# Issuing every second transfer of a layer border from ScalarE, with the Relu on VectorE

## The chip, the cores and the metric

The kernel runs on one core of one Trainium2 chip. A core has TensorE (matrix products, whose results go to the accumulator banks called PSUM), VectorE, ScalarE and GpSimd for elementwise work, SyncE for issuing transfers, and 16 DMA engines that bring data from the chip's memory (HBM) to the on-chip memory (SBUF, 128 partitions). Each engine works through its own list of instructions in order; they meet through semaphores. SyncE and ScalarE can both issue transfers; the profile calls their queues q1 and q10.

The metric is the time of one execution in device microseconds, the median of several runs. The changed kernel is compared with this one.

## What is computed

Two layers over a batch of two single tokens (decoding), each an attention block over a long cache and a gated feed-forward block. The second layer uses the same weights and the same cache as the first.

```python
def _A_ref(x, k_cache, v_cache, wq, wo):          # x: 2 x 1 x 512
    q = (x @ wq) -> 32 heads of 128
    k, v = each of 8 cached heads serves 4 query heads   # cache: 2 x 8 x 32768 x 128, each
    p = softmax(q k^T * 128 ** -0.5)
    return (p v) @ wo
def _B_ref(x, W_gate, W_up, W_down):              # 512 -> 1792 -> 512
    gate = x @ W_gate; gate = gate * (gate > 0)
    return (gate * (x @ W_up)) @ W_down

x = x + _A_ref(_layernorm(x), ...); x = x + _B_ref(_layernorm(x), ...)   # twice
```

All data are fp32. Each layer reads the whole cache of keys and values, 16 groups (8 heads by 2 tokens) of 16 MB of keys and 16 MB of values, except for the part that the second layer finds still on the chip.

## The kernel before

**Places on the chip.** One large SBUF tile, `arena`, holds nearly everything. Its first three parts, X, Z and Y, are slots of 16384 columns (8 MB) for one half of a group's keys or values each. Behind them, partly over the end of Y, lies a **ring** (`RING`) of 6752 columns, 3.46 MB, through which the small weight transfers of the border pass. `ring(width)` gives the next place and begins again at the start when the end is reached.

**The laps.** In a layer, 16 laps each take one group: keys in two halves, a softmax (`soft_max`, whose Exp is ScalarE's work), values in two halves. The second layer takes the groups in the opposite order, so that the key half that the first layer had last can be used again.

**The border.** Between the last lap of the first layer and the first of the second lies a chain that needs little data but in strict order: the last values, the output projection, the feed-forward block, and the queries of the next layer. `feed_forward` reads the weights `wgu` (gate and up) in 32 units of 448 columns, the first 16 for the gate and the others for up, cut into pieces by `UNITS[0]` = 4, 3, 3, 3, 1, 3, 3, 2, 1, 3, 1, 2, 3 units; then `wd` (down) in pieces by `DOWN[0]` = 4, 3, 3, 3, 1 blocks of 512 columns. `queries` then reads `wq` in 17 pieces by `QUERY`, 3, 2, 2, 2, 2, 1 and so on, 32 blocks of 512 columns. Each piece goes to the ring, so its transfer waits until TensorE has used what lay there. After the queries the rest of the kept key half is completed by the four `AGAIN` transfers (line 661).

**Who issues.** `fetch` (line 353) records one transfer. A caller may name the semaphore (`lane`); if not, the next of 16 lanes is taken and the counter `turn[2]` goes up by one. All transfers are SyncE's (line 358), but for the two loads of x at the start, which are ScalarE's (line 372). `turn` (line 339) is the list of counters: place in `stat`, place in the ring, lanes, start of the ring.

**The order around the change.** Every instruction is recorded on a `Tape`, which works out for each one which semaphores it has to wait for: what wrote its inputs, and what still reads the place it writes. What an engine has waited for already is not waited for again. Each engine then runs its own list in the recorded order. Line 214 is where every recorded instruction is given out, so nearly all rows of the profile bear that line, and tiles tell the work apart.

**The Relu.** In `feed_forward`, after the 16 gate units (`e == 15`, line 582), the gate's sums in the bank `acc` are scaled by the layer norm's factor `rs` and cut at zero by one ScalarE instruction (line 583) into `gh`. The up sums, in the bank `op`, are multiplied on by VectorE after all 32 units (line 586). Between, TensorE runs a few matmuls of constants into idle banks (`warm`).

Of the kernel before, what the change touches and what calls it, by code (L numbers as in the profile page):

```python
# [6 lines left out]
AF = mybir.ActivationFunctionType  # L7
ALU = mybir.AluOpType
# [11 lines left out]
FS = F // 4  # L20
# [13 lines left out]
X, Z, Y, FLOW = 0, ROW, 2 * ROW, 3 * ROW  # L34
# [3 lines left out]
RING = Y + ROW - STASH, FLOW + 3840  # L38
# [18 lines left out]
UNITS = (4, 3, 3, 3, 1, 3, 3, 2, 1, 3, 1, 2, 3), (16, 8, 8)  # L57
# [251 lines left out]
def attention_reglu_decode(nc, hold, x, k, v, wq, wo, wgu, wd, out):  # L309
    tape = Tape(nc)  # L310
    pe, dve, act, pool, sp = map(tape.engine, ("tensor", "vector", "scalar", "gpsimd", "sync"))
# [17 lines left out]
    def tile(at, width):  # L329
        return arena[:, at : at + width]  # L330
# [5 lines left out]
    mhalf, mean_cols = cst[:, C_HALF : C_HALF + NB], cst[:, C_MEAN : C_MEAN + 1]  # L336


    turn = [0, FLOW, 0, RING[0]]

    def one():
        turn[0] = (turn[0] + NB) % 32
# [5 lines left out]
    def ring(width):  # L348
        at = turn[1] if turn[1] + width <= RING[1] else turn[3]
        turn[1] = at + width  # L350
        return at

    def fetch(at, src, lane=None, also=()):
        t = arena[:, at : at + src.shape[-1]]
        if lane is None:
            lane = f"lane{turn[2] % LANES}"
            turn[2] += 1
        sp.dma_start(t, src, lane=lane, also=also)
        return t

    def half(src, n, h, at, also=()):
# [28 lines left out]
    def warm(width, bank=acc):  # L390

        pe.matmul(bank[:32, :width], pair, mean_cols.to_broadcast([P, width]), start=True, stop=True)
# [31 lines left out]
    def spread(tot, rows, w, start, stop):  # L424
        for c in range(4):
            pe.matmul(tot[32 * c : 32 * c + rows.shape[-1], :P], rows, w[:, c * P : (c + 1) * P], start=start, stop=stop)
# [137 lines left out]
    def feed_forward(last, total):  # L564
        xT, ss = centred(total, not last)
        gh, hT = tile(WIDE_AT, FS), tile(XT_AT, FS)
        up = acc, op
        begins = {sum(UNITS[last][:e]): n for e, n in enumerate(UNITS[last])}
        for e in range(8 * KT):
            if e in begins:  # L570
                n = begins[e]
                t, at = fetch(X + e * FS if last else ring(n * FS), wgu[:, e * FS : (e + n) * FS]), e
            s, kt, j = e // 16, e // 4 % 4, e % 4
            pe.matmul(up[s][32 * j : 32 * j + 32, :FS], xT[:, kt, :], t[:, (e - at) * FS : (e - at + 1) * FS],
                      start=kt == 0, stop=kt == KT - 1)
            if e == 3:
                rs = factor(ss, True)
            if last and e in (15, 23):
                warm(448, scores[:, 0, :])
            elif not last and e in (23, 27):  # L580
                warm(224)
            if e == 15:
                act.activation(gh, up[0][:, :FS], AF.Relu, scale=rs[:, 0:1])
        warm(448)
        for a, e in ((0, 256), (256, FS)):
            dve.scalar_tensor_tensor(gh[:, a:e], up[1][:, a:e], rs[:, 0:1], gh[:, a:e], ALU.mult, ALU.mult)
            dve.transpose(hT[:, a:e], gh[:, a:e])
        rows = hT.rearrange("p (a b) -> p a b", b=32)
        tot = small[1]
        c = 0  # L590
        for n in DOWN[last]:
            t = fetch(Z + c * D if last else ring(n * D), wd[:, c * D : (c + n) * D])
            for e in range(c, c + n):
                spread(tot, rows[:, e, :], t[:, (e - c) * D : (e - c + 1) * D], e == 0, e == NC - 1)
            c += n
            if c in ((4, 8) if last else (4, 7, 10)):
                warm(448)
            elif last and c in (10, 12):
                warm(224)
        return add(tot, last)  # L600
# [3 lines left out]
    for L in range(NLAYER):  # L604
        last = L == NLAYER - 1
        step = -1 if last else 1
        seq = list(range(NG))[::step]


        a, c, b = (X, Z, Y) if not last else (Z, X, Y)  # L610

        weights, other = [tile(WO_AT + at * WO, WO) for at in ((1, 0) if last else (0, 1))]

        def keys(h, t, first=0, scores=scores):
            for e in range(0, t.shape[-1] // D, 8):
                k_blocks(h + e, t[:, e * D : min(t.shape[-1], (e + 8) * D)], first, scores)
                yield e

        def values(lo, t, first=False, final=False):
            n = t.shape[-1] // D  # L620
            for e in range(0, n, 8):
                v_blocks(lo + e, lo + min(e + 8, n), t[:, e * D : min(e + 8, n) * D], first and e == 0, final and e + 8 >= n)

        def lap(i, second, k_first):

            values(HALF, second or half(v, seq[i - 1], 1, b), False, True)
            evacuate(False)
            for e in keys(0, k_first or half(k, seq[i], 0, a, (weights,) if i > L else ())):
                if e == 8:
                    head_out(1, tile(ACS_AT, D), weights)  # L630
            if not last and i == NG - 1:
                pool.tensor_copy(tile(RING[1], KEPT), tile(a, KEPT))
            for _ in keys(HALF, half(k, seq[i], 1, c)):
                pass
            soft_max()
            soft_tail()
            values(0, half(v, seq[i], 0, a), True)
            place_queries(seq[L] + step, step)
            if i % 2 == 1 and i > 1 and (last or i + 1 < NG):
                h = seq[i] // NB  # L640
                if h == 0:
                    fetch_out(h, 1, weights)
                elif i % 4 == 3:
                    fetch_out(h - last, 2, tile(WO_AT, 2 * WO))
                else:
                    pool.tensor_copy(weights, other)

        kept = keys(HALF, tile(a, ROW), NT // 2, gu) if last else iter(())
        queries(L, total, seq[0], kept)
        dve.memset(oT, 0.0)  # L650
        for _ in kept:
            pass
        nothing(op, True)
        ready = {}
        if last:
            n, e = divmod(KEPT, D)

            def again(col):
                return a + col - KEPT if col < REST * D else RING[0] + LENT + col - REST * D

            for lo, hi in AGAIN:
                fetch(again(lo), k[seq[0], 0, :, lo:hi])
            k_blocks(0, tile(RING[1], n * D), NT // 2, gu)
            k_blocks(n, tile(RING[1] + n * D, e), NT // 2, gu, (0, e))
            k_blocks(n, tile(again(KEPT), D - e), NT // 2, gu, (e, D))
            for lo in range(n + 1, HALF):
                for _ in range({12: 3, REST: 2, 26: 2}.get(lo, 0)):
                    warm(448)
                if lo == REST + 4:
                    put_back(LENT, STASH)  # L670
                k_blocks(lo, tile(again(lo * D), D), NT // 2, gu)
            ready = {1: (tile(b, ROW), half(k, seq[1], 0, a))}
            fetch_out(seq[0] // NB, 1, weights)
            warm(448)
            warm(448)
            soft_max(gu)
            soft_tail()
            values(0, tile(c, ROW), True)
            place_queries(seq[1])
        else:  # L680
            ready = {0: (tile(b, ROW), None)}
            fetch_out(0, 1, weights)
            dve.memset(tile(PT_AT, 2 * D), 0.0)
            nothing(acc, True)
        for i in tape.laps(range(L, NG), 1):
            lap(i, *ready.pop(i, (None, None)))
        nothing(op, False)
        combine()
        n = seq[NG - 1]
        for lo, hi in ENDING if last else FLOWN:  # L690
            t = fetch(b + lo * D, v[n, 1, :, lo * D : hi * D])
            if not last and hi == TAIL:
                v_halves(HALF + lo, t)
            else:
                values(HALF + lo, t, False, last and lo >= 28)
            if not last and lo == TAIL:
                for at, bank in stash():
                    dve.tensor_copy(bank, tile(RING[0] + at, bank.shape[-1]))
        if not last:
            warm(SPARE[1], small[1])  # L700
            warm(SPARE[1], small[1])
        head_out(n % NB, evacuate())
        if not last:
            warm(SPARE[1], small[1])
        project(weights if last else fetch_out(n // NB, 1, tile(ring(WO), WO), None), True)
        total = feed_forward(last, add(op))
    sp.dma_start(out, xq, lane="out")
    tape.write()
# [30 lines left out]
```

## Time and profile before

| | |
|---|---|
| median of three runs | 2558.35 us (2557.49 to 2558.69) |
| the profiled execution: own time, span in the trace | 2558.98 us, 2557.7 us |
| granted TensorE clock over the span | 0.751 |
| busy: TensorE, VectorE, ScalarE, GpSimd | 52%, 6%, 2%, 1% |
| bytes read | 1102.76 MB |
| chain that ended last: waiting for keys, for values | 37%, 34% |
| the border: the first `wgu` piece issued, last `wq` piece issued | 1272.23 us, 1325.20 us |
| ScalarE: last Exp before the border, Relu, next Exp | 1252.27, 1292.47, 1352.95 us |

A row of the groups and of the timeline names a line, an engine, an operation, and its result and inputs by tile (`acc<-arena` is a product of data in `arena` into the bank `acc`); `x64` is the count. SPq and ACTq are instructions of SyncE and ScalarE that issue transfers; their time is that of the issue, not of the transfer. A time in square brackets is how long the engine had stood idle before that row, and for whom. In a list of waits the three numbers are the total in us, how many times, and the longest. In the rows of issues stand the count, the size of each, and the median time from issue to the last byte's landing. "DMA share" is the mean busy share of the 16 DMA engines; a packet is counted where it starts, so in a short window the share can be a little over 1.

### The profile page before, as it was taken

How to read it: one execution, taken by the hardware profiler on the slowest of the kernel's cores; microseconds unless marked ns; L12 is line 12 of the kernel's file. 1: busy time of each engine (PE TensorE's matmuls, PEld its weight loads, DVE VectorE, ACT ScalarE, POOL GpSimd, SP SyncE). 2: the span in 40 equal slices, each digit the busy share in tenths (PEclk: the TensorE clock that was granted, in tenths of full speed). 3: DMA queues.
4: the chain of work that ended last, by engine and by line, in shares of the span. 5: the costliest groups of instructions: out<-in, count | busy, mean ns of one | idle time of the engine just before them, and what ended most of it. 6: DMA issues, size and time to landing. Idle time of an engine off the chain costs nothing.

```text
span 2557.7 us, 20577 instructions
## 1 busy us (share of the span) xinstructions
PE 1337.5 (52%) x9546; PEld 366.1 (14%) x9546; DVE 156.3 (6%) x405; ACT 60.3 (2%) x82; POOL 18.5 (1%) x25
## 2 busy tenths in 40 slices
PE   4554545455444554455586554455545554455456
PEld 1111111111111111111121111111111111111112
DVE  1000000000000000000111000000000000000001
ACT  0000000000000000000000000000000000000000
POOL 0000000000000000000000000000000000000000
PEclk9677777777776777777798777777777777777778
DMA  9999999999999999999999999999999999999999
GB/s 425 429 440 428 437 430 436 434 429 440 429 440 427 438 430 430 439 429 440 420 403 440 432 436 431 433 436 431 437 430 437 430 434 435 433 436 431 437 430 390
DMA packets 27391, 1103.06 MB, mean 431 GB/s; under 512 B 3048, under 2 KB 3568, under 8 KB 8304
## 3 DMA queue, kind: packets, MB, share of 16 engines
q1 hardware_dynamic: 27360, 1102.84, 99.9%
q8 instruction: 12, 0.20, 0.0%
q14 instruction: 3, 0.02, 0.0%
q10 hardware_dynamic: 16, 0.00, 0.0%
HBM read 1102.76 MB, written 0.07 MB: 431 GB/s over the span
## 4 chain that ended last, share of the span: by engine, by line
DMA 73%; PE 25%; issue 0%; SPq 0%; DVE 0%; ACT 0%; ACTq 0%
DMA arena<-k 37%; DMA arena<-v 34%; PE acc L214 12%; PE pair L214 11%; DMA arena<-wd 1%; PE op L214 1%; PE small L214 1%; DMA arena<-wq 1%; DMA arena<-wgu 0%; SPq L214 0%; DVE arena L214 0%; DVE stat L214 0%; DVE xq L214 0%; ACT arena L214 0%; ACTq L295 0%
## 5 line engine op out<-in xcount | busy, mean ns | idle before, releaser
L214 PE MATMUL acc<-arena 128*16 128x512 f32 (+2 forms) x4292 | 612.7, 726 | 530.7 <-DMA arena<-v 519.9
L214 PE MATMUL pair<-arena,qz 128*32 128x512 f32 x4098 | 593.8, 732 | 557.9 <-DMA arena<-k 557.9
L214 PEld LDWEIGHTS pair<-arena,qz 128*32 128x32 f32 x4098 | 151.8, 131 | 989.0 <-issue 702.1
L214 PEld LDWEIGHTS acc<-arena 128*16 128x16 f32 (+1 forms) x4292 | 136.9, 112 | 970.2 <-issue 594.9
L214 ACT ACTIVATE arena<-pair,stat 128x1024 f32<-128x1024 f32 x32 | 35.6, 1113 | 2390.2 <-DVE stat L214 2390.2
L214 DVE TENSOR_SCALAR arena<-acc,stat 128x512 f32<-128x512 f32 (+2 forms) x35 | 25.0, 719 | 1049.0 <-PE acc L214 1049.0
L214 DVE TENSOR_REDUCE stat<-pair 128x1 f32<-128x1024 f32 x32 | 39.2, 1224 | 635.9 <-PE pair L214 635.9
L214 DVE STREAM_TRANSPOSE arena<-arena 128x512 f32<-128x512 f32 (+1 forms) x68 | 43.4, 674 | 40.8 <-ACT arena L214 40.7
L214 PE MATMUL small<-stat,cst 128*128 128x1 f32 (+1 forms) x72 | 17.0, 305 | 48.6 <-ACT arena L214 48.6
L214 PE MATMUL small<-arena,cst 128*128 128x32 f32 x64 | 13.1, 287 | 51.6 <-DVE arena L214 51.6
L214 PEld LDWEIGHTS small<-cst,arena 128*128 128x128 f32 x264 | 31.9, 191 | 29.5 <-issue 27.3
L214 PE MATMUL small<-cst,arena 128*128 128x4 f32 x264 | 34.8, 255 | 1.1 <-DVE arena L214 1.1
L214 PE MATMUL op<-arena,oT 128*2 128x512 f32 (+1 forms) x312 | 34.4, 526 | 0.4 <-DVE oT L214 0.3
L214 DVE MEMSET oT<- 128x8 f32 x33 | 2.1, 65 | 513.0 <-PE op L214 513.0
L214 POOL COPY arena<-arena 128x2048 f32<-128x2048 f32 (+1 forms) x7 | 13.8, 1972 | 2191.8 <-PE op L214 2046.8
L214 PE MATMUL op<-arena 128*32 128x448 f32 (+1 forms) x128 | 22.9, 573 | 4.2 <-DMA arena<-wgu 2.0
L214 PEld LDWEIGHTS small<-stat,cst 128*128 128x128 f32 x72 | 13.9, 242 | 56.9 <-ACT arena L214 52.2
L214 PEld LDWEIGHTS small<-arena,cst 128*128 128x128 f32 x64 | 9.5, 188 | 80.5 <-DVE arena L214 80.5
L214 ACT ACT_TABLE_LOAD x16 | 20.5, 1283 | 11.2 <-DMA xq<-x 10.9
L214 PE MATMUL acc<-cst 128*32 128x448 f32 (+1 forms) x48 | 18.3, 480 | 0.0
L214 PE MATMUL small<-cst,stat 128*128 128x2 f32 x8 | 1.7, 287 | 18.4 <-DVE stat L214 17.8
L214 PE MATMUL small<-arena 128*32 128x128 f32 x224 | 8.7, 277 | 2.8 <-DMA arena<-wd 2.2
(63 smaller groups left out, 98.9 us busy)
## 6 DMA issues: line engine op xcount, KB each, us to landing
arena<-wo SPq DMA_DIRECT2D x6, 2048.0 KB, 31.9
arena<-v SPq DMA_DIRECT2D x2, 4096.0 KB, 37.8
arena<-wq SPq DMA_DIRECT2D x13, 512.0 KB, 6.2
arena<-wgu SPq DMA_DIRECT2D x7, 672.0 KB, 6.3
arena<-wo SPq DMA_DIRECT2D x4, 1024.0 KB, 25.7
arena<-wgu SPq DMA_DIRECT2D x1, 3584.0 KB, 44.7
arena<-wgu SPq DMA_DIRECT2D x2, 1792.0 KB, 49.0
arena<-v SPq DMA_DIRECT2D x2, 1536.0 KB, 41.9
```

Source lines behind the costliest of these rows:

```text
L214: ins = getattr(engine, op.call)(*args, **op.kw)
```

## The change

Three things are changed. `turn` gets a fifth entry, a switch, which `feed_forward` puts on in the first layer when it reaches the fifth piece of `wgu` (`sum(UNITS[0][:4])` is unit 13), and which is put off just ahead of the `AGAIN` transfers. While it is on, `fetch` gives a transfer without a lane of its own to ScalarE when the lane counter is odd, else to SyncE as before. And the Relu, in both layers, is a VectorE instruction: times `rs`, then the larger of that and zero.

```diff
-    turn = [0, FLOW, 0, RING[0]]
+    turn = [0, FLOW, 0, RING[0], False]
...
     def fetch(at, src, lane=None, also=()):
         t = arena[:, at : at + src.shape[-1]]
+        by = sp
         if lane is None:
             lane = f"lane{turn[2] % LANES}"
             turn[2] += 1
-        sp.dma_start(t, src, lane=lane, also=also)
+            if turn[4] and turn[2] % 2:
+                by = act
+        by.dma_start(t, src, lane=lane, also=also)
         return t
...
         for e in range(8 * KT):
+            if e == sum(UNITS[0][:4]):
+                turn[4] = not last
             if e in begins:
                 n = begins[e]
                 t, at = fetch(X + e * FS if last else ring(n * FS), wgu[:, e * FS : (e + n) * FS]), e
...
             if e == 15:
-                act.activation(gh, up[0][:, :FS], AF.Relu, scale=rs[:, 0:1])
+                dve.tensor_scalar(gh, up[0][:, :FS], rs[:, 0:1], 0.0, ALU.mult, ALU.max)
...
+            turn[4] = False
             for lo, hi in AGAIN:
                 fetch(again(lo), k[seq[0], 0, :, lo:hi])
```

## The prediction

> **What bounds the kernel now.** I read the page first: where the bytes go, and the chain that ended last.
>
> ```profile
> q1 hardware_dynamic: 27360, 1102.84, 99.9%
> ...
> q10 hardware_dynamic: 16, 0.00, 0.0%
> HBM read 1102.76 MB, written 0.07 MB: 431 GB/s over the span
> ...
> DMA 73%; PE 25%; issue 0%; SPq 0%; DVE 0%; ACT 0%; ACTq 0%
> ```
>
> One queue, SyncE's (q1), keeps the 16 DMA engines busy for 99.9% of the span; q10, which carried only the two loads of x, is ScalarE's. The kernel is a stream of bytes, so an edit counts only if the DMA engines stand idle, or take longer over the same bytes, for more or less time than now.
>
> Next I cut the trace into windows: a stretch of the steady laps, then the border between the layers. The last two columns are the busy share of the DMA engines and their GB/s.
>
> ```profile
> core 0: us, PE busy (x) PEld busy (x) DVE busy (x) ACT busy (x) POOL busy (x), PEclk, DMA share, GB/s
> 1100.00:1178.00 78.00, 38.82 (x276) 10.38 (x276) 4.76 (x13) 3.04 (x4) 0.00 (x0) 0.76 1.00 432
> 1288.00:1296.00 8.00, 5.48 (x32) 0.87 (x26) 0.00 (x0) 0.63 (x1) 0.00 (x0) 1.00 1.00 382
> 1316.00:1320.00 4.00, 3.42 (x16) 0.57 (x14) 0.38 (x1) 0.00 (x0) 0.00 (x0) 1.00 0.96 326
> 1330.00:1344.00 14.00, 13.42 (x92) 4.45 (x88) 1.20 (x4) 0.00 (x0) 0.00 (x0) 1.00 1.00 415
> 1283.00:1330.00 47.00, 37.74 (x330) 11.93 (x321) 7.01 (x27) 0.63 (x1) 1.26 (x2) 1.00 1.01 399
> ```
>
> The changed issues lie between 1283 and 1330. There the engines are busy as everywhere (1.01), yet move 399 GB/s against 432. Only 1316 to 1320 shows a share under 1 (0.96) and 326 GB/s: the one place where the queue looks almost empty. This gives the **most the change can bring**. The 47 us moved 47 x 399 = 18.75 MB, which at 432 GB/s take 43.4 us, 3.6 less; the 14 us at 415 would take 13.45, 0.55 less. Together 4.15 us, 0.16% of the time. The first bound lies inside what a measurement of this kernel can tell from no change, about 0.2% or 5.1 us.
>
> What holds the border's transfers back is in the waits of SyncE between 1283 and 1330: for whom, us in total, times, longest.
>
> ```profile
> SPq L214 <- PE op L214: 22.3, 13, 5.9
> SPq L214 <- PE acc L214: 7.9, 8, 1.4
> SPq L214 <- PE small L214: 7.6, 6, 1.9
> SPq L214 <- PE pair L214: 2.3, 1, 2.3
> ```
> SyncE waits 22.3 + 7.9 + 7.6 + 2.3 = 40.1 of the 47 us for TensorE to free a place of the ring; TensorE, busy 37.74, is idle 9.3 of them, as it uses each piece once it lands. It is a circle: land, use, free, issue, land. Only when its round is too long for the bytes in flight do the DMA engines run dry.
>
> **The change, part by part.** The moved part is 9 gates' pieces (19 units of 224 KB), 5 of `wd` (14 of 256 KB) and 17 of `wq` (32 of 256 KB): 31 transfers, 16,032 KB. The lane counter stands at 11 on the first, so the odd ones go to ScalarE: 16 transfers. SyncE keeps 15.
>
> First, the time of an issue. Where one release of TensorE frees two places, SyncE now issues them one behind the other.
>
> ```profile
> 1283.41 0.80 SPq L214 DMA_DIRECT2D arena<-wgu  x2
> ```
> ```profile
> 1315.01 0.80 SPq L214 DMA_DIRECT2D arena<-wq  x2
> ```
> ```profile
> 1283.41 0.33 SPq L214 DMA_DIRECT2D arena<-wgu  x1
> ```
>
> There are seven such couples between 1283 and 1325, the first and the last shown, each about 0.8 us long. One issue that waited takes 0.33 us, so the second stands some 0.4 us behind the first, and with two issuers it need not. It gains only where the DMA engines are waiting for it, which the windows show at 1316 to 1320 alone, right behind the couple of 1315.01. Value: **-0.4 us**; ends: 0 and 7 x 0.4 = -2.8.
>
> Second, the order in which data land. Now a piece lands whole before the next one begins. With two queues on the same engines the pieces may come by turns. The only traffic on q10 in this trace shows it.
>
> ```profile
> 1.08 9.67 ACTq L214 DMA_DIRECT2D xq<-x  x2
> ```
> ```profile
> q10 hardware_dynamic: 4, 0.00, 0.7%
> ```
> ```profile
> q10 hardware_dynamic: 4, 0.00, 0.5%
> ```
>
> The second row is of the window 7 to 8 us (the four data rows of 512 B), the third of 9.5 to 10 (the four small completion writes); from 8 to 9.5 nothing of q10 started. So 1 KB issued at 1.08 is done only near 10, and a big row of SyncE's queue came in between its data and its completion write. This is taking turns row by row. Two equal pieces that start together then land together, at the end of both: the earlier is late by up to its own length, and in a steady alternation by half of it. A 512 KB piece takes 1.31 us at 399 GB/s and one of 672 KB 1.72, so half is **0.66 to 0.86 us**.
>
> Is that covered? From issue to landing, median, and the shortest of the border (issued into the empty moment at 1315.01):
>
> ```profile
> arena<-wq SPq DMA_DIRECT2D x13, 512.0 KB, 6.2
> arena<-wgu SPq DMA_DIRECT2D x7, 672.0 KB, 6.3
> ```
> ```profile
> arena<-wq SPq DMA_DIRECT2D x1, 512.0 KB, 4.4
> ```
>
> A usual piece spends 6.2 - 4.4 = 1.8 us standing in the queue. A landing that is 0.66 to 0.86 later eats under half of this, so the engines still find work; it is hidden, except at the dry moment, where one half piece, **+0.7 us**, is paid. An issue by ScalarE may also be longer than SyncE's: the one row of it is of small transfers.
>
> ```profile
> L214 ACTq DMA_DIRECT2D xq<-x x2: 514/802/1090, 1.1 to 10.2; - x2
> ```
>
> That is 0.18 to 0.76 us over 0.33. With 0.86 it comes to 1.62, still under 1.8: nothing where there is a queue.
>
> [...]
>
> Third, the border's end. The first transfer of the kept-over key half (1712 KB) now stands on SyncE behind the last `wq` piece.
>
> ```profile
> 1325.20 0.33 SPq L214 DMA_DIRECT2D arena<-wq  x1
> ```
> ```profile
> 1325.57 0.43 SPq L214 DMA_DIRECT2D arena<-k  x1
> ```
> ```profile
> arena<-k SPq DMA_DIRECT2D x1, 1712.0 KB, 9.2
> ...
> arena<-k SPq DMA_DIRECT2D x1, 1536.0 KB, 16.4
> ```
> ```profile
> 1340.57 2.76 PE L214 MATMUL pair<-arena,qz 128*32 128x512 f32 x18 [0.58 <-DMA arena<-k]
> ...
> 1348.77 1.48 PE L214 MATMUL pair<-arena,qz 128*32 128x512 f32 x10 [1.56 <-DMA arena<-k]
> ```
>
> With that piece on ScalarE, the key transfer no longer waits behind it. It has eight rows per engine of 13,696 B against eight of 4,096, so by turns the piece could land behind all of it: 1712 KB / 399 GB/s = 4.4 us late at worst. TensorE has 0.58 + 1.56 = 2.1 us of waiting in store behind it. The rest delays only the softmax; the DMA engines hold keys by then (the 1536 KB take 3.9 us by rate and land after 16.4, so 12 us of queue), and nothing is paid in bytes: 0, at worst +2.3.
>
> Fourth, the Relu, once in each layer.
>
> ```profile
> 1292.47 0.63 ACT L214 ACTIVATE arena<-acc,stat 128x448 f32<-128x448 f32 x1 [38.99 <-PE op L214]
> ```
> ```profile
> L214 DVE TENSOR_SCALAR arena<-acc,stat 128x512 f32<-128x512 f32 x31 | 23.3, 750 | 1033.1 <-PE acc L214 1033.1
> L214 DVE TENSOR_SCALAR arena<-acc,stat 128x384 f32<-128x384 f32 x2 | 1.2, 617 | 15.8 <-PE acc L214 15.8
> ```
> ```profile
> DVE arena L214 <- PE op L214: 14.4, 1, 14.4
> ```
> ```profile
> DVE arena L214 <- PE op L214: 7.8, 1, 7.8
> ```
>
> Halfway between the VectorE rows, 128x448 takes about 0.68 us against 0.63. VectorE then waits 14.4 us (first layer) and 7.8 us (second) for the up half, so it is hidden: 0. Without that cover it would be 0.05. It also clears ScalarE: left there, it would stand between the transfers, as ScalarE takes its instructions in order. Nothing else of ScalarE's lies among them: it had idled 38.99 us before that Relu, and its next Exp needs the keys behind the border.
>
> **Sum**: -0.4 + 0.7 + 0 + 0 = +0.3 us on the profiled execution, 2558.98 to 2559.3. That execution lies 0.63 above the median of the three runs (2558.35), so the forecast is 2558.35 + 0.3, about **2558.6**.
>
> **The rivals.** (a) *The second queue fills the slow moments*: with two queues an engine has another row at hand whenever one arrives late. For it: a share of 1.00 at 382 GB/s, so the rows themselves are slow. Against it: half the pieces still come only when TensorE frees a place. It can win back at most the 4.15; half, -2.1, gives 2556.3.
>
> (b) *The round becomes too long* (the slower side): pieces by turns land half a piece later, and if the 1.8 us of standing are not there every round pays. Bytes in flight are 399 GB/s x 6.2 us = 2.47 MB, so 18.75 MB are 7.6 rounds; times 0.66 to 0.86 that is 5.0 to 6.5, mean 5.8: 2564.1. It decides from the point at which the time from issue to landing falls to 4.4 us plus the delay. For it: only 382 GB/s at 1288 to 1296. Against it: a share of 1.00 there. [...]
>
> (c) *The change does not do what it says*: each transfer waits for TensorE anyway, so two issuers are no faster than one and turns cost nothing: 2558.35.
>
> **How the numbers follow.** The forecast (from -1 to +1.5 around now) 0.50, (c) 0.14, (a) 0.19, (b) 0.17. Faster by over 0.2% would need more than the 4.15 us: 0.03. Of (b) about half lies beyond +5.1: slower 0.08. Within 0.2%: 0.89. The range takes in most of (a) and the milder part of (b): -2.9 to +4.2 around the median, 2555.5 to 2562.5.
>
> **What would show each step.** The queue rows: q10 with some 8.4 MB (8,160 KB). The windows: 1316 to 1320 over 326 GB/s if the couple counted, 1288 to 1296 near 382 if turns are hidden; both above 400 proves (a), and a share under 0.95 in several windows proves (b). The landing times: by turns, `wq` and `wgu` pieces go from 6.2 to about 7, the last `wq` piece far more, and the first key transfer is issued before 1325. The VectorE Relu should take 0.68 us with no one waiting. It would all be wrong if the end moved by over 5 us: then some lap outside the border has changed, which no row here foresees.

## The result, and the profile after

The changed kernel takes **2569.04 us** (median of 5 runs, 2568.13 to 2571.89) against 2558.35 (median of 5, 2557.49 to 2562.27) for the kernel before on the same chip: 10.7 us or 0.42% slower, ratio 1.0042 with a 95% interval of 1.0028 to 1.0057. The forecast was 2558.6, in a range of 2555.5 to 2562.5, with 0.08 on slower by over 0.2%.

The page of the changed kernel shows the transfers on the two queues as intended: 8.36 MB on ScalarE's q10.

```profile
q1 hardware_dynamic: 25056, 1094.48, 98.8%
q10 hardware_dynamic: 2320, 8.36, 0.9%
```

Where the time went is read from two windows, first of the kernel before, then of the changed one (columns as above; the last two are the DMA share and GB/s).

```profile
1288.00:1344.00 56.00, 46.88 (x368) 14.63 (x366) 6.78 (x22) 0.63 (x1) 0.70 (x1) 1.00 1.01 401
1344.00:1360.00 16.00, 11.78 (x73) 3.49 (x69) 5.39 (x11) 1.21 (x2) 0.00 (x0) 0.89 1.04 447
```
```profile
1288.00:1344.00 56.00, 36.00 (x306) 12.58 (x302) 7.36 (x22) 0.00 (x0) 0.70 (x1) 0.92 0.99 378
1344.00:1360.00 16.00, 16.00 (x93) 5.11 (x88) 3.17 (x7) 0.00 (x0) 0.00 (x0) 0.96 0.67 264
```

Up to 1344 the DMA engines stay busy but move 378 GB/s instead of 401: 56 x 23 = 1.29 MB less, 3.0 us at the steady 432. From 1344 to 1360 they are idle for a third of the time and move 16 x 183 = 2.93 MB less, 6.8 us. Together 9.8 us; the spans differ by 9.9 (2567.6 and 2557.7). Nothing outside this stretch is needed to explain the result. In the second window TensorE, which had waited before, is busy for all 16 us: the stream has run out because TensorE is late and the next transfer waits for it.

Why it is late shows in the timelines and issues of the changed kernel: the last `wq` piece, ScalarE's; TensorE's wait for it; and when SyncE issues the last of the four key transfers and the next 8 MB key half.

```profile
1330.05 0.34 ACTq L214 DMA_DIRECT2D arena<-wq  x1
```
```profile
arena<-wq ACTq DMA_DIRECT2D x1, 512.0 KB, 10.8
```
```profile
1340.87 1.07 PE L214 MATMUL acc<-arena 128*32 128x512 f32 x2 [5.41 <-DMA arena<-wq]
```
```profile
1342.83 0.33 SPq L214 DMA_DIRECT2D arena<-k  x1
```
```profile
1354.46 0.33 SPq L214 DMA_DIRECT2D arena<-k  x1
```

Before, the piece was issued at 1325.20 and landed 5.5 us later; the next key half was issued at 1343.37:

```profile
arena<-wq SPq DMA_DIRECT2D x1, 512.0 KB, 5.5
```
```profile
1343.37 0.33 SPq L214 DMA_DIRECT2D arena<-k  x1
```

Now the piece is issued 4.85 us later and takes 10.8 us instead of 5.5, so TensorE goes on some 10 us later. SyncE's waits in the changed kernel show what hangs on it: from 1334.2 to 1343 the last of the four key transfers waits for TensorE's query products (`acc`; 2.2 us before), and from 1343.2 to 1354.7 the next key half waits for the key products behind them (`pair`; 10.7 us before).

```profile
SPq L214 <- PE acc L214: 8.7, 1, 8.7
```
```profile
SPq L214 <- PE pair L214: 11.3, 1, 11.3
```

So the next key half is issued 11.1 us later. The rows that passed while the piece was in flight, counted by queue from 1334 to 1337.4:

```profile
q1 hardware_dynamic: 83, 1.07, 76.5%
q10 hardware_dynamic: 83, 0.34, 25.3%
```

83 rows of one queue and 83 of the other. Of SyncE's, 15 are small completion writes (the view counts 15 packets under 512 B) and the others rows of 13,696 and 18,432 B; ScalarE's are all rows of 4,096 B. The queues went on by equal counts and not by equal bytes: the piece got 0.34 MB of 1.41, a quarter. That the turns are single rows is shown at the run with the last piece alone.

### The profile page after: what moved, and what is told of

Same layout as the page of the kernel before. It is cut to its first block, busy times and chain, and to the rows that moved or that the text cites. A ratio compares the mean times of both kernels' runs of the same rounds, so it can differ in the third digit from the quotient of the medians.

```text
span 2567.6 us, 20577 instructions
## 1 busy us (share of the span) xinstructions
PE 1338.6 (52%) x9546; PEld 368.7 (14%) x9546; DVE 157.8 (6%) x407; ACT 59.1 (2%) x80; POOL 18.5 (1%) x25
## 3 DMA queue, kind: packets, MB, share of 16 engines
q10 hardware_dynamic: 2320, 8.36, 0.9%
## 4 chain that ended last, share of the span: by engine, by line
DMA 74%; PE 25%; issue 0%; SPq 0%; DVE 0%; DVEq 0%
DMA arena<-k 38%; DMA arena<-v 33%; PE pair L214 11%; PE acc L214 11%; DMA arena<-wgu 2%; PE op L214 1%; PE small L214 1%; DMA arena<-wq 1%; DMA arena<-wd 0%; SPq L214 0%; DVE arena L214 0%; DVE xq L214 0%; DVEq L212 0%; SPq L212 0%
## 5 line engine op out<-in xcount | busy, mean ns | idle before, releaser
L214 DVE TENSOR_SCALAR arena<-acc,stat 128x512 f32<-128x512 f32 (+3 forms) x37 | 26.4, 718 | 1055.5 <-PE acc L214 1048.9
L214 ACT ACT_TABLE_LOAD x16 | 20.5, 1283 | 11.6 <-DMA xq<-x 11.3
```

Of the source, the lines that this page charges most:

```text
L214: ins = getattr(engine, op.call)(*args, **op.kw)
```

## The experiments

Each is compared with the kernel before on the same chip (2557.86 to 2558.18 in these series); `dve`, `act` and `sp` are VectorE, ScalarE and SyncE. Differences are between medians, with the interval of the ratio. Single runs of kernels with two queues scatter by several us, so the windows and landing times belong to the one profiled execution, the prices to the medians.

**The Relu alone on VectorE.** The kernel before, with one line:

```diff
-                act.activation(gh, up[0][:, :FS], AF.Relu, scale=rs[:, 0:1])
+                dve.tensor_scalar(gh, up[0][:, :FS], rs[:, 0:1], 0.0, ALU.mult, ALU.max)
```


> The kernel before with the Relu on VectorE alone; all transfers stay SyncE's. Theory of the rows taken in turn (the whole loss comes from two queues sharing the DMA engines): 2558.4 us, within 1 us of before, as VectorE waits 6 us or more for the up half behind it. Rival (the Relu on VectorE delays the chain of the border or of the end): 2559.5 or more.

Measured 2557.63 against 2557.86, ratio 1.0 (0.9991 to 1.0009): the Relu is not the cause.

**The last `wq` piece given back to SyncE**, the other 15 left to ScalarE:

```diff
                     n = begins[4 * e + c]
+                    if 4 * e + c + n == 8 * KT:
+                        turn[4] = False
```


> The changed kernel with the last wq piece alone given back to SyncE, so that it stands in one queue ahead of the first key transfer; the other 15 stay ScalarE's. Theory A (the large loss is the end of the border: the last wq piece shares the engines row by row with the 13.7 and 18.4 KB key rows, TensorE is late, the next key half is issued late and the DMA queue runs empty around 1351 to 1355): the dry moment goes, and the 3.0 us that the border lost up to 1344 stay, 2561 to 2563. Theory B (the loss is the lateness gathered in gates, down and queries, which starves the queue anyway): 2566 or more.

2563.99, +6.1 us (1.0015 to 1.0034): between the ranges of the two theories. One transfer of 512 KB makes 4.6 us of the 10.7. Its two windows show that the dry moment is gone (451 GB/s) while the first stretch is as slow as in the changed kernel (379 beside 378):

```profile
1288.00:1344.00 56.00, 43.73 (x348) 13.62 (x346) 7.47 (x23) 0.00 (x0) 0.70 (x1) 0.94 0.98 379
1344.00:1360.00 16.00, 12.35 (x72) 3.82 (x68) 5.40 (x11) 1.21 (x2) 0.00 (x0) 0.92 1.06 451
```

Theory A holds for the end of the border, but 6.1 is twice the 3.0 that it left to the rest; so both theories name a part. (The profiled execution of this kernel, 2561.38, was the fastest of its ten runs, the slowest 2567.46.)

**The even lanes instead of the odd ones**, so that the last piece is SyncE's without further edit:

```diff
-            if turn[4] and turn[2] % 2:
+            if turn[4] and turn[2] % 2 == 0:
```


> The changed kernel with the even lanes instead of the odd ones on ScalarE: 15 transfers, the last wq piece is SyncE's, the piece ahead of it (256 KB) ScalarE's. Theory A: as much mixing inside the border but none of a wq piece of 512 KB with key rows, 2561 to 2564. Theory B: the lateness inside the border decides, 2566 or more, as in the changed kernel.

2563.57, +5.7 us (1.0013 to 1.0031), as the run before it.

**All 31 on ScalarE:**

```diff
-            if turn[4] and turn[2] % 2:
+            if turn[4]:
```


> The changed kernel with all 31 transfers on ScalarE: no two queues side by side inside the border, but several wq pieces are still waiting on ScalarE's queue when the first key transfer is issued by SyncE, perhaps earlier than now. Theory A (the meeting of wq rows with key rows decides): the last three or four wq pieces each lose turns to key rows, the last lands 10 us or more late, 2568 to 2576. Theory B (alternation inside the border decides): nothing is mixed there, 2558 to 2562.

2563.83, +6.0 us (1.0014 to 1.0033): between the two expectations, so the time alone decides nothing, but its windows do.

```profile
1296.00:1308.00 12.00, 9.26 (x128) 4.10 (x132) 1.61 (x4) 0.00 (x0) 0.00 (x0) 1.00 1.02 418
1308.00:1320.00 12.00, 10.09 (x64) 2.36 (x54) 2.71 (x11) 0.00 (x0) 0.70 (x1) 1.00 1.02 399
...
1344.00:1352.00 8.00, 8.00 (x51) 2.70 (x50) 2.32 (x4) 0.00 (x0) 0.00 (x0) 1.00 0.44 157
```

With one queue the border runs as well as before (418 and 399 GB/s, where it was 421 and 381); the changed kernel had 394 and 338 in these stretches:

```profile
1296.00:1308.00 12.00, 6.60 (x84) 2.98 (x84) 1.61 (x4) 0.00 (x0) 0.00 (x0) 1.00 1.00 394
1308.00:1320.00 12.00, 8.54 (x90) 3.47 (x90) 2.62 (x10) 0.00 (x0) 0.70 (x1) 1.00 0.97 338
```

All of its loss is the dry moment at 1344 to 1352 (share 0.44), behind a last piece that took 10.6 us to land. The several late pieces of theory A were not seen: its last piece alone met the keys.

**Gates and down alone by turns; queries alone by turns.** The first puts the switch off ahead of the queries; the second puts it on there, and off for the last piece, and has no switch in `feed_forward`:

```diff
+        turn[4] = False        # first run; second: turn[4] = L > 0
         if L == 0:
             whole, begins = fetch(Y, wq, f"slot{Y // ROW}"), {}
```


> The changed kernel with the switch put off again ahead of the queries: every second gates' and down piece by ScalarE, all of wq by SyncE, so no wq piece meets key rows. The run with only the last wq piece given back stood 6.1 us over before; this asks where these 6 arise. Theory C (each stretch pays by its number of mixed pieces, 14 of 31 here): +2 to +3.5, 2560 to 2561.5. Theory D (it is the third and fourth down pieces landing together, ahead of the chain of layer norm and queries, that delays everything behind): +4 to +6, 2562 to 2564.

> Alternation in the queries alone, the last wq piece left to SyncE: 8 of 17 wq pieces by ScalarE, gates and down all SyncE's. Theory C: +2.5 to +4, 2560.5 to 2562. Theory D: within 1.5 us of before, 2558 to 2559.5.

2561.93, +3.75 us (1.0004 to 1.0022), and 2563.29, +5.1 us (1.0010 to 1.0029). Both stretches pay, so theory D, by which the queries alone would cost nothing, falls. Both medians lie a little over theory C's ranges, and 3.75 + 5.1 = 8.9 is more than the 6.1 of both together; but the intervals, 1.0 to 5.6 us and 2.6 to 7.4, hold C's ranges too and leave open whether the prices add.

**One queue to the end**, ScalarE's: also the four key transfers and the next 8 MB key half, so that SyncE takes over where much is queued.

```diff
-            if turn[4] and turn[2] % 2:
-                by = act
+        if turn[4]:
+            by = act
...
-            turn[4] = False
             for lo, hi in AGAIN:
...
             ready = {1: (tile(b, ROW), half(k, seq[1], 0, a))}
+            turn[4] = False
```


> One queue, but ScalarE's: from the fifth gates' piece on every transfer of the border, the four key transfers behind the queries and the next 8 MB key half are all ScalarE's; SyncE takes over where tens of us of data are queued. No small piece meets large rows. Theory of turns at the handover (the 6 us of the run with all 31 on ScalarE come from the last wq piece and the first key transfer in two queues, nothing from ScalarE as issuer): no dry moment at 1344 to 1352, 2556 to 2559, no slower than before. Rival (issuing from ScalarE itself costs, or its lateness): 2562 or more again.

2558.44, +0.26 us (0.9995 to 1.0013). ScalarE as an issuer cost nothing that can be seen here; it is the two queues side by side that did.

**Shorter key rows.** The changed kernel, its first key transfer in four, with rows of 3,424 B:

```diff
-            for lo, hi in AGAIN:
+            cut = (12 * D - KEPT) // 4
+            for lo, hi in (*((KEPT + e * cut, KEPT + (e + 1) * cut) for e in range(4)), *AGAIN[1:]):
```


> The changed kernel with the first key transfer (1712 KB, rows of 13,696 B) cut into four of 428 KB (rows of 3,424 B). Theory of turns row by row: eight wq rows of 4 KB now pass eight key rows of 3.4 KB instead of 13.7 and 18.4 KB, so the last wq piece lands 7 us or less after its issue instead of 10.8, and the time falls most of the way to the run with that piece on SyncE, 2563 to 2566. Rival (the queues share by bytes or by whole transfers, so row size does not matter; or the lateness before it decides): the last piece still lands 9 us or more after its issue, 2568 to 2570.

2564.90, +6.7 us (1.0018 to 1.0041), and the last piece:

```profile
arena<-wq ACTq DMA_DIRECT2D x1, 512.0 KB, 7.0
```

Both figures are in the ranges of the theory of turns row by row. The profiled execution, to which the 7.0 belongs, took 2559.92, the shortest of the seven and 5 us under their median, so the cleaner test of this theory is the pair with the last piece alone, below.

**The Relu left on ScalarE, between the transfers** (the changed kernel with the old line):

> The changed kernel with the Relu back on ScalarE, so ScalarE's list is transfers, Relu, transfers. If the move of the Relu is there to keep the transfers from standing behind it: pieces of ScalarE after unit 15 wait for the gate's matmuls to end (about 1292.4), but these pieces wait for places freed at about that time or later anyhow: within 1.5 us of the changed kernel, 2567.5 to 2570.5. Rival (it holds up the pieces): 2571 or more.

2571.51, 2.5 us above the changed kernel's 2569.04, though the two intervals overlap (this one is 1.0042 to 1.0070). That is over the range expected and in the rival's, and the trace shows its mechanism, though not its price: behind the Relu four pieces stand and go out together at 1293.03; in the changed kernel ScalarE issues its five one by one from 1283.63 on.

```profile
1293.01 0.63 ACT L214 ACTIVATE arena<-acc,stat 128x448 f32<-128x448 f32 x1 [40.23 <-PE op L214]
1293.03 2.07 ACTq L214 DMA_DIRECT2D arena<-wgu  x4
```
```profile
1283.63 9.73 ACTq L214 DMA_DIRECT2D arena<-wgu  x5
```

**One change of issuer ahead of the queries**: gates from the fifth piece on and down by ScalarE, all of `wq` by SyncE.

> The gates' pieces from the fifth on and all of down by ScalarE, all queries by SyncE: the issuer changes once from ScalarE to SyncE where rows are of like size (6,144 and 4,096 B), in place of by turns. Theory of turns: only the pieces in flight at the change are mixed, so at most 1.5 us over before, 2557.5 to 2559.7. Rival (ScalarE's pieces ahead of the layer norm cost whatever the order, as in the run with 14 alternating gates' and down pieces, 2561.9): 2561 or more.

2560.95, +3.0 us (1.0005 to 1.0023): over the 2559.7 that the theory allowed, and at the rival's bound of 2561. Here the last down piece (rows of 2,048 B) meets `wq` rows of 6,144 B; from 1308 to 1311 SyncE's queue moved 1.00 MB and ScalarE's 0.22, and the piece landed 7.7 us after its issue; 5.7 in the kernel before. The counts of that window, 199 and 111, are no equal turns, so that the piece lost its time by turns is argued here, not shown:

```profile
q1 hardware_dynamic: 199, 1.00, 80.9%
q10 hardware_dynamic: 111, 0.22, 18.8%
```
```profile
arena<-wd ACTq DMA_DIRECT2D x1, 256.0 KB, 7.7
```
```profile
arena<-wd SPq DMA_DIRECT2D x1, 256.0 KB, 5.7
```

**The last `wq` piece alone on ScalarE**, everything else SyncE's; then the same with the shorter key rows:

```diff
                     n = begins[4 * e + c]
+                    turn[4] = 4 * e + c + n == 8 * KT
```

`fetch` tests `turn[4]` alone here, and `feed_forward` has no switch.

> One transfer alone by ScalarE: the last wq piece, 512 KB; everything else SyncE's, the Relu on VectorE. Theory A: it meets the first key transfer on the other queue, lands 4 us or more later than before, the next key half is issued as much later and the DMA queue runs empty behind the key transfers: 2561.5 to 2564.5. Rival (the handover only hurts where the border is late already): 2558 to 2560.

> As the run with the last wq piece alone by ScalarE, and the first key transfer cut into four with rows of 3,424 B. Theory of turns row by row: the piece passes the small rows, lands 7 us or less after its issue, and there is hardly a dry moment: 2557.5 to 2560. Rival (any meeting of two queues costs the same): 2561.5 or more, as without the cut.

2562.70, +4.7 us (1.0007 to 1.0025), and 2557.50, -0.5 us (0.9991 to 1.0009). The landing of that piece in the two, and the issue of the next key half:

```profile
arena<-wq ACTq DMA_DIRECT2D x1, 512.0 KB, 10.5
```
```profile
1345.99 0.33 SPq L214 DMA_DIRECT2D arena<-k  x1
```
```profile
arena<-wq ACTq DMA_DIRECT2D x1, 512.0 KB, 7.5
```
```profile
1342.91 0.33 SPq L214 DMA_DIRECT2D arena<-k  x1
```

This is the cleanest pair of the study. One transfer of the kernel's 1103 MB, on time and in a border that is not late, costs 4.7 us on the other queue (2.4 in the profiled execution, 2560.35); cutting its neighbour's rows, not moving it back, takes the cost away. The 7.5 us are a little more than was expected of the piece, the time is what was expected.

In the run without the cut, from 1329 to 1331, no packet is under 512 B, so that only data rows are counted:

```profile
q1 hardware_dynamic: 48, 0.66, 76.9%
q10 hardware_dynamic: 48, 0.20, 23.9%
```

48 rows of one queue and 48 of the other. By the shares, one of SyncE's rows took 0.51 us (76.9% of 16 engines' 2 us, divided by 48) and one of ScalarE's 0.16. The start times in the trace show that the turns are single rows: eight of the piece's rows, as many as one engine has, start at 1327.11, 1327.77, 1328.44, 1329.10, 1329.76, 1330.43, 1331.09 and 1331.75, each 0.66 us behind the last, which is one key row and one of its own. Of the piece's 128 rows 101 have another 0.66 us behind them. Eight turns of 0.51 us make the piece some 4.1 us later, by estimate; it landed 5.0 us later than in the kernel before (10.5 and 5.5).

**The change of issuer one piece earlier.** What stayed open was the price inside the border. As the run with one change of issuer, but the last down piece is SyncE's too:

```diff
         for n in DOWN[last]:
+            if c + n == NC:
+                turn[4] = False
```


> As the run with gates and down by ScalarE and the queries by SyncE (2560.95), but the change of issuer comes one piece earlier: the last down piece (256 KB, rows of 2,048 B) is SyncE's too, so it stands in one queue ahead of the wq pieces (rows of 6,144 B). Theory of turns: the 3 us there came from this piece losing turns to wq rows (7.7 us from issue to landing against 5.7 before), late ahead of the chain of layer norm; now 2557.5 to 2559.7. Rival (a change of issuer at this place costs whatever the rows): 2560.3 or more.

2558.86, +0.75 us by the medians, where the run one piece later had +3.0. The interval, 0.9995 to 1.0032, is wide, as one of the eleven runs took 2586.94 us, at a granted clock of 0.595 over its span where the others had about 0.75. The medians go with the theory; the interval does not exclude the rival, and the landing does not bear the theory out: in the profiled execution (2561.04, 2.2 us over the median) the piece, now SyncE's, still took 7.4 us.

```profile
arena<-wd SPq DMA_DIRECT2D x1, 256.0 KB, 7.4
```

So what the change of issuer costs inside the border, and by which piece, stays open.

**`wq` in 32 pieces of one block, by turns (the last one SyncE's) and, as a control, all by SyncE:**

```diff
-QUERY = 3, 2, 2, 2, 2, 1, 2, 2, 2, 2, 1, 2, 2, 2, 2, 1, 2
+QUERY = (1,) * 32
```


> Alternation in the queries alone with the last piece on SyncE, as in the run that gave 2563.3, and wq cut into 32 pieces of 256 KB instead of 17. Read against the same cutting with all pieces on SyncE. Theory of turns (a piece is late by about half of the piece beside it): at most 2.5 us over that control. Rival (two queues side by side cost the same whatever the size of the pieces): 4 us or more over it.

> Control for the run with wq in 32 pieces: the kernel before with the Relu on VectorE and the same cutting, all by SyncE. More and shorter rows and more issues: 2558 to 2561.

2557.07 by turns and 2556.97 by SyncE: 0.1 us apart, where the pieces of 512 KB paid 5.1. The medians of both are 1 us under before, but not beyond their intervals (0.9991 to 1.0009 and 0.9987 to 1.0026, the latter again with one run of 2587.13 at a clock of 0.595); the control was expected at 2558 or more. Alternation of 256 KB pieces with equal rows cost nothing that can be seen here; of the longer ones it did, as the theory of turns has it.

**A version to hold against both kernels:** all by SyncE, `wq` in 32 pieces and the first key transfer in four.

> A candidate for beating both kernels: all transfers SyncE's, the Relu on VectorE, wq in 32 pieces of 256 KB and the first key transfer in four. Theory of the ring's round (smaller pieces free their places and land sooner): as the run with the cut wq or a little under it, 2555.5 to 2557.5, against 2558 for before. Rival (the extra rows cost what the sooner landing brings): 2557.5 to 2559.

2557.16 against 2557.89, ratio 0.9998 (0.9989 to 1.0007): clearly better than the changed kernel, and not told apart from the kernel before.

## Why the prediction was wrong

*Right:* the bound on the gain (no kernel's median lay more than 1.2 us under before); the Relu (0.685 us measured, 0.68 worked out, and no change in time); 8.36 MB on q10 for 8.4. The second issue of a couple did go out earlier, at 1288.74 beside SyncE's 1288.69 instead of 0.4 us behind; no gain in time from it can be seen in any run. Two of the named signs also came, 381 GB/s at 1288 to 1296 and 346 at 1316 to 1320, and misled: the stretch between them, 1308 to 1316, for which no sign was named, fell from 409 to 334. The first key transfer was issued at 1329.37, not before 1325.

```profile
1288.69 0.33 SPq L214 DMA_DIRECT2D arena<-wgu  x1
```
```profile
1288.74 0.35 ACTq L214 DMA_DIRECT2D arena<-wgu  x1
```

ScalarE's issue took 0.35 us, not the 0.51 to 1.09 of the x loads, so that rival price was nothing.

*The step that failed most* is the third part, the border's end: "0, at worst +2.3", on the ground that "the DMA engines hold keys by then". It measured 4.7 us alone and 4.6 in the changed kernel. The lateness was seen and bounded (the piece "could land behind all of" the key transfer, 4.4 us; it took 5.3 us longer). What was missing is whom the late piece holds up: the last key transfer waits for TensorE's product with that piece, the rest of the kept keys stands behind that product in TensorE's order, and the next 8 MB key half waits for those key products. The cover was read off one transfer, the 1536 KB with 12 us of queue, when the transfer that mattered was the next one. Before, that key half was issued at 1343.37, and the last key transfer ahead of it (issued at 1332.29, 16.4 us to landing) lasted until 1348.7: a reserve of 5 us, not 12, against a delay of 11.1.

```profile
1332.29 0.33 SPq L214 DMA_DIRECT2D arena<-k  x1
```

*The second part* was the right mechanism at the wrong size: half a piece of 0.66 to 0.86 us, "hidden, except at the dry moment", +0.7 in all. It measured +5.1 for the queries, +3.75 for gates and down, +6.1 for both. Two things were off. Half a piece is an average, and the 1.8 us of standing in the queue, a median, were taken as a reserve at every round. The third down piece, on SyncE, landed 8.4 us after its issue at 1301.22 instead of 6.4, more than that reserve, just ahead of the chain of layer norm and queries. Its equal on ScalarE, issued at 1301.59, landed within 0.2 us of it, so this piece was late by the whole length of its neighbour: 768 KB at 399 GB/s are 1.97 us. Where the rows are unequal, as for the query piece beside keys, a piece pays for its neighbour's row at each turn, which was more still: the last piece alone landed 5.0 us later. Nor were the pieces of one queue as neatly parted before as the prediction had it: in that trace the last rows of the last `wq` piece (4,096 B) started at 1330.24, and the first of the key transfer behind it (13,696 B) at 1328.74.

```profile
arena<-wd SPq DMA_DIRECT2D x1, 768.0 KB, 8.4
```
```profile
arena<-wd ACTq DMA_DIRECT2D x1, 768.0 KB, 8.2
```
```profile
arena<-wd SPq DMA_DIRECT2D x1, 768.0 KB, 6.4
```

These rows are the changed kernel's on SyncE and on ScalarE, and the kernel before's. So rival (b) was nearest to what happened, and its sum (5.0 to 6.5 us for the rounds) is about what the border's inside cost. That agreement is partly luck: the median landing of the 512 KB `wq` pieces issued between 1283 and 1330 rose from 6.2 to 6.5 (ScalarE's) and 6.8 (SyncE's), less than the 0.66 to 0.86 of every piece, and up to 1344 no window named had a share under 0.95, the sign of (b). The prediction had all parts add to +0.3, where these two make some 6 and 4.6.

On the turns: a piece of 512 KB is 128 rows of 4,096 B for 16 engines, eight each. The equal counts of 48 and 48, the row starts 0.66 us apart, and the landing that falls from 10.5 to 7.5 us with shorter neighbour rows show turns of one row, as the prediction had read them off the x rows. The saving in issue time that it counted on was not seen, and the second issuer cost 10.7 us. The run with one queue on ScalarE (+0.26 us) shows that the cost lies not with the issuer.

*What stays open:* how the 6.1 us inside the border divide (3.75 and 5.1 by the parts alone, with wide intervals), and why the single runs of kernels with two queues lie up to 9 us apart, where those of the kernel before lie 2 to 6 apart. Nor are size of piece and length of row told apart inside the border: the 32 pieces of `wq` are smaller and have short, equal rows.

## What to carry to other kernels

In these runs two issuing engines were two queues that shared the DMA engines row by row: a transfer with short rows lost to one with long rows (10.5 us to landing instead of 5.5). Keep transfers that are needed in order in one queue (ScalarE's to the end: +0.26 us), or give them rows of like length and small size (-0.5 us for the last piece beside key rows of 3,424 B, 0.1 us for `wq` in 32 pieces by turns); change the issuer only where no one waits for the next piece (+0.26 us at the 8 MB key half, +3.0 ahead of the queries). And when a delay is priced at nothing because the stream has work queued, find the last transfer that waits for the delayed engine, and compare the delay with what is in flight at that transfer.

## What the runs showed of the hardware that was not expected

In the run with the last piece alone on ScalarE, an engine with work on two queues took one row of each in turn (48 and 48 rows in 2 us, and eight rows of one queue at steps of 0.66 us), so that the queue with rows of 4,096 B got 0.20 MB while the other got 0.66. And the granted TensorE clock, 1.00 from 1288 to 1344 before, fell to 0.83 and 0.80 in the stretches where TensorE waited for late pieces:

```profile
1320.00:1330.00 10.00, 7.41 (x42) 2.92 (x46) 1.36 (x4) 0.00 (x0) 0.00 (x0) 0.83 1.00 372
1330.00:1344.00 14.00, 8.59 (x64) 2.47 (x56) 1.09 (x3) 0.00 (x0) 0.00 (x0) 0.80 1.00 402
```

The run with the last piece alone on ScalarE went dry with a clock of 1.00 in both stretches, so the lower clock is not needed for it:

```profile
1320.00:1330.00 10.00, 9.84 (x73) 3.30 (x76) 1.08 (x4) 0.00 (x0) 0.00 (x0) 1.00 1.03 415
1330.00:1344.00 14.00, 10.25 (x75) 3.16 (x69) 1.20 (x4) 0.00 (x0) 0.00 (x0) 1.00 1.01 430
1344.00:1352.00 8.00, 8.00 (x42) 2.41 (x37) 3.54 (x5) 0.00 (x0) 0.00 (x0) 1.00 0.74 281
```

It added to the lateness in the changed kernel, though. There the clock stood at 0.50 just behind the wait for the last piece, and 14 key products took 4.10 us; in the run with the last piece alone 14 took 2.30:

```profile
1340.00:1344.00 4.00, 3.13 (x16) 0.78 (x18) 1.09 (x3) 0.00 (x0) 0.00 (x0) 0.50 0.99 420
1341.73 4.10 PE L214 MATMUL pair<-arena,qz 128*32 128x512 f32 x14
```
```profile
1335.07 2.30 PE L214 MATMUL pair<-arena,qz 128*32 128x512 f32 x14
```

From TensorE's first product with the late piece to the issue of the next key half the two kernels took 13.6 us (1340.87 to 1354.46) and 11.4 us (1334.60 to 1345.99). So some 2 of the 11.1 us of delay go with the lower clock, an estimate from two kernels; no run holds the clock alone apart.
